# Seven block products in place of eight for half of an output product, in batches 3 to 7

## The chip, the cores and the metric

The kernel runs on one core of a Trainium2 chip. A time is the device time of one execution in microseconds; the time of a kernel is the median over its runs. The profile is of one more execution, taken by the hardware profiler: its span runs from the first to the last instruction. The engines are TensorE (PE, with its weight loads as PEld), VectorE (DVE), ScalarE (ACT), GpSimd (POOL) and SyncE (SP), which issues nearly all transfers.

## What is computed

Random-feature attention for 8 batches of 8 heads (576 tokens, 64 wide), and after it a dense two-layer network over the 4608 tokens that come out:

```
phi(x) = exp(h - max(h)) / sqrt(128),  h = omega x - |x|^2/2
attention = phi(q) (phi(k)^T v) / (phi(q) sum phi(k) + 1e-6)
h = x @ w_in              # 512 -> 2048 (d_ff)
g = h * erf(softplus(h))
out = g @ w_out           # 2048 -> 512
```

Everything is fp32. TensorE is given each number as a high part (rounded to fp32r) and the rest; a product is three matmuls, high x high, high x rest and rest x high.

## The kernel before

Tokens are worked on by batch (576 tokens, as two halves of T = 288), d_ff by two phases of 1024. A matmul has a 128x128 weight and a moving operand of 128x288. A phase (b, ph) has four steps `f0` to `f3`, each making 256 rows of h (a tile hs of 2 row blocks x 2 token halves), and four steps `e0` to `e3` that make the output product of the *phase before*, 128 output rows each. `BLOCKS` gives their order: f0 f1 e0 f2 e1 f3 e2 e3. From batch 2 on the first product (`gemm1`, with the table `PRODUCTS`) is done by a Strassen-like scheme: seven products of blocks in place of eight, with sums of the inputs (tiles xc, split into xh and xl) and of the weights (`make_sums`, tiles wS). The names hA.. and hS.. are PSUM tiles of these seven products; DVE and ACT add them into hs. The output product (`gemm2`, PSUM tiles o..) is plain: for each of 4 output blocks, 2 token halves and 8 row blocks of d_ff three matmuls, 192 in a phase.

Between them stands `chain`: after two steps f, ACT makes softplus and erf of two tiles hs (gs, with a table load ahead of each function), then hs is multiplied by gs (the gate, on DVE or POOL), rounded into gh (DVE or ACT), and the rest hs - gh goes into gl (POOL or DVE).

The program is written down by a planner (`Plan.order`). It gives each operation a due time, counts back from the matmuls with costs written into the source, and lets each engine take the most urgent ready operation; what comes out is one fixed list for each engine. On the chip each engine works through its list in order, and waits by semaphores. Tiles lie in pools of slots (`SLOTS`): 8 for weights (512 KB each, fetched again from device memory for every use), 6 each for gh and gl, 4 for hs, 8 PSUM banks. `CAPS` limits how many PSUM banks one kind of product holds: 3 for h, 2 for o, 6 for the attention.

The attention for later batches (names ppk, ppq, kvp, pt, nd on PE; unk, unq, fk, fq, qh, ql, kh, kl, xs elsewhere) is put between these steps. Batch 7 has none left beside it. In the profile nearly all instructions have line 866, that of the helper which records them; one reads it by tile names.

Of the kernel before, what the change touches and what calls it, by code (L numbers as in the profile page):

```python
# [62 lines left out]
LAG = {"T": 0.35, "A": 0.35, "V": 0.33, "G": 0.33, "S": 0.3}  # L63
SLOTS = dict(w=8, u=2, un=2, f=2, mx=2, sq=2, v=2, qh=1, ql=1, kh=2, kl=2, xs=4, xh=2, xl=2, u2=2,
             hs=4, gs=2, gh=6, gl=6, os=4, ps=8)
# [6 lines left out]
SHARED = ("wrest", "wshift", "wwhole", "wsum", "xsum", "xhigh", "xrest", "gate",  # L72
          "high", "rest")

# [247 lines left out]

BLOCKS = (("f", 0), ("f", 1), ("e", 0), ("f", 2), ("e", 1), ("f", 3), ("e", 2), ("e", 3))
WHOLE = 12
PLAIN = 2
# [29 lines left out]
def build(emit):  # L355
# [3 lines left out]
    seq = [(b, ph) for b in range(B) for ph in range(NPH)]  # L359
    starts = [START0]  # L360
    for b, ph in seq:
        starts.append(starts[-1] + FP * (STEP2 + (STEP1 if b >= PLAIN else STEP1 * 8 / 7))
                      + (NP * PAIR / 2 if b + 1 < B else 0.0))
# [21 lines left out]
    def fetch(u, t, src):  # L385
        pl.op("wfetch", [("S", 0.1, AHEAD)], lambda e: E.fetch(t.ap.bitcast(F32), src()),
              reads=[(stored[u], 0)], writes=[(t, (x, k)) for x in "hl" for k in range(t.shape[1])],
              size=P * t.shape[1] * BW * 8)

    def store(u, t):  # L390
        d = stored[u] = pl.tile("wd" + t.name, "wd" + t.name, t.shape)
        pl.op("wstore", [("S", 0.1, 1e9)], lambda e: E.fetch(d.ap, t.ap.bitcast(F32)),
              reads=[(t, (x, k)) for x in "hl" for k in range(2)], writes=[(d, 0)],
              plan=clock[0] + 10.0, size=P * HW * 8)
# [43 lines left out]

    def make_sums(ph, fp, t0, t1):

        r = pl.tile("gh", f"R{ph}_{fp}", [P, 2, 2, BW], F32, "sr", 1)
# [4 lines left out]
        s = pl.tile("gl", f"S{ph}_{fp}", [P, 4, BW], F32, "ss", 1)  # L446

# [282 lines left out]
    def gemm1(b, ph, fp):  # L730
        where = weights1(b, ph, fp)
        hs = pl.tile("hs", f"hs{b}_{ph}_{fp}", [P, 2, 2, T])
        gran[b, ph, fp] = {"hs": hs}
        u2 = pl.tile("u2", f"u2{b}_{ph}_{fp}", [P, T])

        def place(x):
            return (u2, 0) if x == "U2" else (hs, x)

        def view(x):
            return u2.ap if x == "U2" else hs.ap[:, x[0], x[1], :]  # L740
        for wn, xn, outs in PRODUCTS:
            hp = pl.tile("ps", f"h{wn}{b}_{ph}_{fp}", [P, 512], F32, "moe1")
            product(hp, where, wn, b, XB, xn, 0, 1)
            for to, plus in outs:
                if plus is None:
                    pl.op("hout", [("A", 0.34, -1e9), ("V", 0.38, 0.0)],
                          lambda e, hp=hp, to=to: E.h_out(e, view(to), hp), reads=[(hp, 0)],
                          writes=[place(to)])
                else:
                    pl.op("hadd", [("V", 0.375, -1e9)],  # L750
                          lambda e, hp=hp, to=to, plus=plus: E.h_add(view(to), hp, view(plus)),
                          reads=[(hp, 0), place(plus)], writes=[place(to)])

    macros = [0]

    def chain(b, ph, fps):
# [13 lines left out]
        for fp, g in zip(fps, gr):  # L770
            four = [(g["hs"], (i, t)) for i in range(2) for t in range(2)]
            pl.op("gate", [("V", 1.27, -1e9), ("G", 2.78, GATES if (b, ph) >= EARLY else GATES0)], lambda e, g=g: E.gate(e, g["gs"], g["hs"]),
                  reads=four + [(g["gs"], 0)], writes=four)
            g["gh"] = pl.tile("gh", f"gh{b}_{ph}_{fp}", [P, 2, 2, T], F32R, cap=4 if b < PLAIN or (b, ph) == (PLAIN, 0) else None)
            pl.op("high", [("V", 0.68, -1e9), ("A", 1.08, 3.0)], lambda e, g=g: E.high(e, g["gh"], g["hs"]),
# [3 lines left out]
                  lambda e, g=g: E.rest(e, g["gl"], g["hs"], g["gh"]),  # L779
                  reads=four + [(g["gh"], 0)], writes=[(g["gl"], 0)])  # L780

    def gemm2(b, ph, et):
# [4 lines left out]
        for h in range(2):  # L787
            w = weights2(ph, et, h)
            for t in range(2):
                for fi in range(FT // 2):  # L790
                    f = h * (FT // 2) + fi
                    fp, i = divmod(f, 2)
                    g = gran[b, ph, fp]
                    k = [(w, (x, fi // 2)) for x in "hl"]
                    pl.op("g2", [("T", 3 * COST["mm"], -1e9)],
# [28 lines left out]
    for k, (b, ph) in enumerate(seq):  # L824
        length = starts[k + 1] - starts[k]
        clock[0] = starts[k]
        clock[1] = length / (FP * (STEP2 + STEP1 * (1 if b >= PLAIN else 8 / 7)))
        if not ph:
            for c in range(KH):
                split(b, c)  # L830
        for i, (what, x) in enumerate(BLOCKS):
            if what == "f":
                (plain1 if b < PLAIN else gemm1)(b, ph, x)
                if x % 2:
                    chain(b, ph, (x - 1, x))
# [13 lines left out]
def tile_attention_moe(ctx: ExitStack, tc: tile.TileContext, qT, kT, qN, kN, vP, omT, w1, w2, out):  # L849
# [62 lines left out]
    class Emit:  # L912
# [217 lines left out]
        def gemm2(self, op, w, fi, gh, gl, i, t, f):  # L1130
            b, c = divmod(fi, 2)
            wh, wl = (w.ap[:, b, x, c * P:(c + 1) * P] for x in range(2))
            for x, (l, r) in enumerate(((wh, gh.ap), (wh, gl.ap), (wl, gh.ap))):
                pe.matmul(op.ap[:, :T], lhsT=l, rhs=r[:, i, t, :], start=f == 0 and x == 0,
                          stop=f == FT - 1 and x == 2)

        def o_out(self, e, o, op, t):
# [71 lines left out]
```

## Time and profile before

| | |
|---|---|
| time, median of 3 runs | 1026.38 us (1026.01 to 1029.21) |
| the profiled execution | 1024.2 us, span 1022.4 us |
| busy: PE, PEld | 1005.8 us (98%), 977.8 us (96%) |
| busy: DVE, ACT, POOL | 725.5 us (71%), 688.1 us (67%), 552.3 us (54%) |
| transfers | 254.18 MB, 249 GB/s over the span |
| granted TensorE clock | 1.000 |

Batch 2 begins near 299 us, batch 3 near 420 us, and a batch takes 121.5 us from there to batch 6. Matmuls overlap: one lasts about 0.3 us, but they start 0.13 us apart. A view by windows gives, for each stretch, the busy time of each engine with its instructions, the granted clock, the busy share of the 16 DMA engines and GB/s.

### The profile page before, as it was taken

How to read it: one execution, taken by the hardware profiler on the slowest of the kernel's cores; microseconds unless marked ns; L12 is line 12 of the kernel's file. 1: busy time of each engine (PE TensorE's matmuls, PEld its weight loads, DVE VectorE, ACT ScalarE, POOL GpSimd, SP SyncE). 2: the span in 40 equal slices, each digit the busy share in tenths (PEclk: the TensorE clock that was granted, in tenths of full speed). 3: DMA queues.
4: the chain of work that ended last, by engine and by line, in shares of the span. 5: the costliest groups of instructions: out<-in, count | busy, mean ns of one | idle time of the engine just before them, and what ended most of it. 6: DMA issues, size and time to landing. Idle time of an engine off the chain costs nothing.

```text
span 1022.4 us, 23095 instructions
## 1 busy us (share of the span) xinstructions
PE 1005.8 (98%) x8784; PEld 977.8 (96%) x8784; DVE 725.5 (71%) x1430; ACT 688.1 (67%) x1321; POOL 552.3 (54%) x532
## 2 busy tenths in 40 slices
PE   7999999999999999999999999999999999999998
PEld 7788899999999999999999999999999999999998
DVE  4889889978786677876686767875668756765531
ACT  7979979878685865676677666876657676453340
POOL 6959979879884353835356342752439212343310
PEclk9999999999999999999999999999999999999999
DMA  8676888887776877768776776776866656667761
GB/s 247 201 273 237 287 287 299 286 320 301 276 245 220 306 253 259 246 226 283 247 240 246 274 266 205 246 265 256 281 217 233 220 181 236 226 244 259 274 228 48
DMA packets 80285, 254.18 MB, mean 249 GB/s; under 512 B 9008, under 2 KB 9776, under 8 KB 80176
## 3 DMA queue, kind: packets, MB, share of 16 engines
q1 hardware_dynamic: 80016, 252.12, 71.2%
q8 instruction: 70, 1.15, 0.4%
q10 hardware_dynamic: 160, 0.59, 0.2%
q14 instruction: 39, 0.32, 0.1%
HBM read 218.07 MB, written 34.60 MB: 247 GB/s over the span
## 4 chain that ended last, share of the span: by engine, by line
PE 91%; ACT 3%; DVE 2%; POOL 1%; DMA 1%; issue 0%; SPq 0%; DVEq 0%; POOLq 0%
PE o L866 39%; PE hS L866 15%; PE hA L866 11%; PE h L866 8%; PE nd L866 5%; PE ppk L866 3%; PE kvp L866 3%; PE ppq L866 3%; PE pt L866 2%; ACT fk L866 1%; ACT gs L866 1%; ACT xs L866 1%; DMA uq<-qT 1%; DVE xs L866 0%; DVE pw L866 0%
## 5 line engine op out<-in xcount | busy, mean ns | idle before, releaser
L866 PE MATMUL o<-gh,w 128*128 128x288 f32 x2048 | 445.4, 299 | 0.2 <-DMA w<-wdw 0.2
L866 PEld LDWEIGHTS o<-gh,w 128*128 128x128 f32 x2048 | 338.4, 188 | 5.5 <-issue 0.4
L866 PE MATMUL o<-gl,w 128*128 128x288 f32 x1024 | 301.8, 295 | 0.0
L866 POOL TENSOR_TENSOR hs<-gs,hs 128x576 f32<-128x576 f32 x78 | 124.3, 1617 | 181.1 <-ACT gs L866 118.9
L866 PEld LDWEIGHTS o<-gl,w 128*128 128x128 f32 x1024 | 192.8, 188 | 0.5
L866 PE MATMUL hS<-xh,wS 128*128 128x288 f32 x768 | 186.9, 298 | 0.2 <-ACT fq L866 0.2
L866 POOL TENSOR_TENSOR gl<-hs,gh 128x576 fp32r<-128x576 f32 x80 | 136.7, 1732 | 36.4 <-ACT gh L866 26.1
L866 PE MATMUL hA<-xh,w 128*128 128x288 f32 x576 | 148.1, 298 | 0.0
L866 PEld LDWEIGHTS hS<-xh,wS 128*128 128x128 f32 x768 | 134.3, 188 | 1.1 <-ACT fq L866 0.5
L866 POOL TENSOR_TENSOR unq<-unq 128x288 f32<-128x288 f32 (+2 forms) x67 | 54.5, 815 | 121.6 <-ACT unq L866 75.4
L866 PE MATMUL h<-xh,w 128*128 128x288 f32 x512 | 117.8, 307 | 2.1 <-ACT w L866 1.1
L866 ACT ACT_TABLE_LOAD x92 | 118.0, 1283 | 2.3 <-PEq L1200 0.7
L866 PE MATMUL hS<-xl,wS 128*128 128x288 f32 x384 | 113.4, 295 | 0.0
L866 ACT ACTIVATE fk<-ppk,mxk 128x128 f32<-128x128 f32 x288 | 77.4, 417 | 52.4 <-DVE mxk L866 52.3
L866 PEld LDWEIGHTS hA<-xh,w 128*128 128x128 f32 x576 | 103.3, 188 | 0.0
L866 ACT ACTIVATE xs<-nd,eps 64x288 f32<-64x288 f32 x128 | 63.9, 499 | 48.1 <-PE nd L866 45.8
L866 PEld LDWEIGHTS h<-xh,w 128*128 128x128 f32 x512 | 85.4, 188 | 5.4 <-DVE w L866 1.6
L866 ACT ACTIVATE gs<-hs 128x1152 f32<-128x1152 f32 x64 | 72.9, 1165 | 18.6 <-DVE hs L866 18.2
L866 PE MATMUL hA<-xl,w 128*128 128x288 f32 x288 | 85.2, 296 | 0.0
L866 ACT ACTIVATE fq<-ppq,mxq 128x128 f32<-128x128 f32 x288 | 78.5, 413 | 4.0 <-DVE mxq L866 2.2
L866 PE MATMUL h<-xl,w 128*128 128x288 f32 x256 | 75.8, 296 | 2.2 <-POOL xl L866 2.2
L866 PEld LDWEIGHTS hS<-xl,wS 128*128 128x128 f32 x384 | 72.3, 188 | 0.0
(106 smaller groups left out, 2033.5 us busy)
## 6 DMA issues: line engine op xcount, KB each, us to landing
w<-wdw SPq DMA_DIRECT2D x176, 512.0 KB, 4.5
wS<-wdcS SPq DMA_DIRECT2D x96, 512.0 KB, 4.4
st<-w SPq DMA_DIRECT2D x32, 512.0 KB, 5.6
wdw<-w SPq DMA_DIRECT2D x32, 512.0 KB, 4.3
w<-wdw SPq DMA_DIRECT2D x48, 256.0 KB, 3.7
v<-vP SPq DMA_DIRECT2D x32, 325.0 KB, 5.7
out<-os SPq DMA_DIRECT2D x31, 288.0 KB, 4.1
wdcS<-cS SPq DMA_DIRECT2D x16, 512.0 KB, 4.9
```

The source lines that it names most:

```text
L866: return tc.keep_in_program_order(method(*args, **kwargs))
```

## The change

In batches 3 to 7 the output product of the first phase (ph = 0) is done by the same scheme of seven block products. `operands` takes the four gated tiles hs of the phase in place, makes 16 sums of 128x288 from them (`bsum`, with two spare tiles t2), and splits seven operands (B11, T2, T3, B21, T1, T4, B22; 4 pieces each) into high (`bhigh`, tiles bh in the pool gh) and rest (`brest`, tiles bl in the pool gl): 28 + 28 pieces. The four `high` and four `rest` of these phases, which work on 128x1152, are left out. `block_product` does one of the seven products for two pairs of output blocks: 12 matmuls each into one PSUM tile (bA.., bS..), which DVE (sometimes ACT) then adds to one or two places of the output tile os. That is 168 matmuls in a phase in place of 192. `CUT` lays products 0 to 2 into e0, 3 into e1, 4 and 5 into e2, 6 into e3; in batch 7 `LASTCUT` has 0 and 1, 2, 3 to 6, none.

The weights of these products come as 512 KB columns (wcA from w_out, wcS from its sums), 14 fetches a phase in place of 8. The sums of w_out are made once, in batch 2 (`column_sums`, four times; tiles ct, RT, ST, cST), and stored. Two of the four tiles hs live in the pools gh and gl for these phases (`LENT`). From batch 3 on h may hold 4 PSUM banks, and a block product 3. In `PRODUCTS` the spare tile U2 is replaced by a place in hs that is not filled yet, in all batches that use it; the number of operations stays the same there.

Three places show how the lists change, all in phase (3, 1). **POOL**, from the gate of the third tile on, before:

```order
L866 TENSOR_TENSOR hs3_0_2_6210<-gs3_0_2_6581,hs3_0_2_6210 128x576 x2
L866 TENSOR_TENSOR xc4_0_6709<-xs_4_0_6072 128x288
L866 TENSOR_TENSOR gl3_0_2_6741<-hs3_0_2_6210,gh3_0_2_6714 128x576 x2
L866 TENSOR_TENSOR unk_5_2_6753<-unk_5_2_6753 128x9x32
L866 TENSOR_TENSOR unk_5_2_6753<-unk_5_2_6753 128x9x16
```

and now (the gate stands right ahead of these rows):

```order
L984 TENSOR_SCALAR bhB113_0_6312<-hs3_0_3_6519 128x288
L984 TENSOR_SCALAR bhB113_0_6312<-hs3_0_2_6293 128x288
L984 TENSOR_TENSOR hs3_0_2_6293<-hs3_0_2_6293 128x288
L984 TENSOR_SCALAR bhT23_0_6797<-t23_0_0_6388 128x288
L984 TENSOR_SCALAR bhT33_0_6811<-hs3_0_0_5982 128x288
L984 TENSOR_TENSOR blT23_0_6823<-t23_0_0_6388,bhT23_0_6797 128x288
...
L984 TENSOR_TENSOR hs3_0_2_6293<-t23_0_2_6918,hs3_0_2_6293 128x288
L984 TENSOR_TENSOR blT23_0_6823<-t23_0_2_6918,bhT23_0_6797 128x288
L984 TENSOR_TENSOR hs3_0_2_6293<-hs3_0_2_6293,t23_0_2_6918 128x288
L984 TENSOR_TENSOR t23_0_3_6979<-hs3_0_3_6519 128x288
```

Where one rest of two halves followed the gate, 16 instructions of 128x288 now stand up to the sum t2 of the fourth tile (t23_0_3): 4 roundings, 8 rests (6 of them at the dots) and 4 sums. **DVE**, where it empties the PSUM tiles of f1, before:

```order
L866 TENSOR_TENSOR hs3_1_1_6873<-hA123_1_1_6888,hs3_1_1_6873 128x288
L866 TENSOR_TENSOR hs3_1_1_6873<-hS13_1_1_6909,hs3_1_1_6873 128x288
L866 TENSOR_TENSOR hs3_1_1_6873<-hS13_1_1_6909,u23_1_1_6883 128x288
L866 TENSOR_TENSOR xs_4_2_6905<-nd_4_2_0_0_6861,xs_4_2_6905 64x288
L866 TENSOR_TENSOR hs3_1_1_6873<-hA223_1_1_6919,hs3_1_1_6873 128x288
```

and now:

```order
L984 TENSOR_TENSOR hs3_1_1_6960<-hA123_1_1_6984,hs3_1_1_6960 128x288
L984 TENSOR_TENSOR blT23_0_6823<-t23_0_3_6979,bhT23_0_6797 128x288
L984 TENSOR_TENSOR hs3_1_1_6960<-hS13_1_1_7005,hs3_1_1_6960 128x288 x2
L984 TENSOR_TENSOR hs3_1_1_6960<-hA223_1_1_7015,hs3_1_1_6960 128x288
L984 TENSOR_REDUCE sqq_10_7044<-unq_5_0_6481 128x9
```

The rest of T2's fourth piece, which needs that sum from POOL and its rounding from ACT, now stands ahead of the emptying of hS1. **PE**, at the beginning of e0, before:

```order
L866 MATMUL hS43_1_1_6928<-xh3_0_5710,wS_1_1_1_135_6722 128x288
L866 MATMUL o3_0_0_0_6935<-gh3_0_0_6253,w2_0_0_0_137_6804 128x288
L866 MATMUL o3_0_0_0_6935<-gl3_0_0_6277,w2_0_0_0_137_6804 128x288
L866 MATMUL o3_0_0_0_6935<-gh3_0_0_6253,w2_0_0_0_137_6804 128x288
L866 MATMUL hS43_1_1_6928<-xh3_1_5720,wS_1_1_1_135_6722 128x288
```

and now, there and further down:

```order
L984 MATMUL hS43_1_1_7023<-xh3_0_5750,wS_1_1_1_135_6799 128x288
L984 MATMUL bA113_0_0_7031<-bhB113_0_6312,wcA1100_137_6890 128x288
L984 MATMUL bA113_0_0_7031<-blB113_0_6342,wcA1100_137_6890 128x288
...
L984 MATMUL bS23_0_1_7124<-bhT23_0_6797,wcS201_140_6947 128x288
L984 MATMUL bS23_0_0_7099<-bhT23_0_6797,wcS200_139_6935 128x288
L984 MATMUL bS23_0_0_7099<-blT23_0_6823,wcS200_139_6935 128x288
L984 MATMUL bS23_0_0_7099<-bhT23_0_6797,wcS200_139_6935 128x288
```

The product with B11 begins where the plain one did; the last rows are the fourth piece of T2, 48 instructions after that beginning, 258 after the last matmul of f3 of the phase before.

The core of the diff (the placing into the loop, the plan of the PRODUCTS and the copies of the old functions are cut):

```diff
+CUT = (0, 3, 4, 6, 7)
+LASTCUT = (0, 2, 3, 7, 7)
+BLOCKS2 = 3
+LENT = ("hs", "gh", "gl", "hs")
+MOE1 = 4
+MOE2 = 3
+SUMS2 = ((0, 1), (0, 5), (1, 1), (1, 5))
...
+    def operands(b, ph):
+        gr = [gran[b, ph, fp] for fp in range(FP)]
+        spare = [pl.tile("t2", f"t2{b}_{ph}_{fp}", [P, T]) for fp in range(FP)]
...
+        def total(to, a, c):
+            for fp in range(FP):
+                (d, dk), (x, xk), (y, yk) = place(to, fp), place(a, fp), place(c, fp)
+                pl.op("bsum", [("V", 0.4, -1e9), ("G", 0.75, 3.0)],
+                      lambda e, d=d, x=x, y=y: E.combine(e, d(), x(), y(), -1), reads=[xk, yk], writes=[dk])
...
+                pl.op("bhigh", [("A", 0.44, -1e9), ("V", 0.28, -1e9), ("G", 0.45, 3.0)],
+                      lambda e, h=h, src=src, fp=fp: E.b_high(e, h, src, fp), reads=[key], writes=[(h, fp)])
+                pl.op("brest", [("V", 0.46, -1e9), ("G", 0.78, 3.0)],
...
+        split("B11", b11)
+        total(b12, b12, b11)
+        total("T2", b22, b12)
+        split("T2", "T2")
+        total(b11, "T2", b11)
+        split("T3", b11)
+        split("B21", b21)
+        total(b21, b21, "T2")
+        split("T1", b12)
+        split("T4", b21)
+        split("B22", b22)
...
+        for ep in range(KT // 2):
+            w = column(ph, ep, wn)
+            op = pl.tile("ps", f"b{wn}{b}_{ph}_{ep}", [P, 512], F32, "moe2", MOE2)
+            for f in range(FP):
+                pl.op("g2", [("T", 3 * COST["mm"], -1e9)],
...
+            elif last and blocks2(*last):
+                cut = CUT if k + 1 < len(seq) else LASTCUT
+                for n in range(cut[x], cut[x + 1]):
+                    block_product(*last, n)
...
+            if b == BLOCKS2 - 1 and (ph, i) in SUMS2:
+                ep, h = divmod(SUMS2.index((ph, i)), 2)
+                column_sums(0, ep, h)
```

More of the change, by code (lines that the diff above doesn't have):

```diff
@@ L72 @@
 SHARED = ("wrest", "wshift", "wwhole", "wsum", "xsum", "xhigh", "xrest", "gate",
-          "high", "rest")
+          "high", "rest", "bsum", "bhigh", "brest")
 class Tl:
@@ L360, in build, with blocks2, length2 @@
     starts = [START0]
+    def blocks2(b, ph):
+        return b >= BLOCKS2 and ph == 0
+    def length2(b, ph):
+        return STEP2 * (7 / 8 if blocks2(b - 1 + ph, 1 - ph) else 1)
     for b, ph in seq:
-        starts.append(starts[-1] + FP * (STEP2 + (STEP1 if b >= PLAIN else STEP1 * 8 / 7))
+        starts.append(starts[-1] + FP * (length2(b, ph) + (STEP1 if b >= PLAIN else STEP1 * 8 / 7))
                       + (NP * PAIR / 2 if b + 1 < B else 0.0))
@@ L751, in gemm1 @@
                           lambda e, hp=hp, to=to, plus=plus: E.h_add(view(to), hp, view(plus)),
-                          reads=[(hp, 0), place(plus)], writes=[place(to)])
+                          reads=[(hp, 0), (hs, plus)], writes=[(hs, to)])
     macros = [0]
@@ new lines, in block_product @@
+    def block_product(b, ph, n):
+        wn, xn, outs = PRODUCTS[n]
+        if n == 0:
+            for et in range(KT):
+                o_sb[b, et] = pl.tile("os", f"os{b}_{et}", [P, 2, T])
+        h, l = gran[b, ph][xn]
+        for ep in range(KT // 2):
[3 more added lines that the diff above has]
+                pl.op("g2", [("T", 3 * COST["mm"], -1e9)],
+                      lambda e, w=w, op=op, f=f: E.block_product(op, w, f, h, l),
+                      reads=[(w, (x, f // 2)) for x in "hl"] + [(h, f), (l, f)], writes=[(op, 0)], plan=at())
+            for to, plus in outs:
+                d = o_sb[b, 2 * ep + to[0]]
+                if plus is None:
+                    pl.op("oout", [("V", 0.38, -1e9), ("A", 0.34, -1e9)],
+                          lambda e, d=d, op=op, to=to: E.o_out(e, d, op, to[1]),
+                          reads=[(op, 0)], writes=[(d, to[1])])
+                else:
+                    p = o_sb[b, 2 * ep + plus[0]]
+                    pl.op("oadd", [("V", 0.375, -1e9)],
+                          lambda e, d=d, p=p, op=op, to=to, plus=plus:
+                          E.h_add(d.ap[:, to[1], :], op, p.ap[:, plus[1], :]),
+                          reads=[(op, 0), (p, plus[1])], writes=[(d, to[1])])
@@ L826, in build @@
         clock[0] = starts[k]
-        clock[1] = length / (FP * (STEP2 + STEP1 * (1 if b >= PLAIN else 8 / 7)))
+        clock[1] = length / (FP * (length2(b, ph) + STEP1 * (1 if b >= PLAIN else 8 / 7)))
         if not ph:
@@ L830, in build @@
                 split(b, c)
-        for i, (what, x) in enumerate(BLOCKS):
+        for i, (what, x) in enumerate(BLOCKS if k + 1 < len(seq) else LASTBLOCKS):
             if what == "f":
@@ L1131, in gemm2 @@
             b, c = divmod(fi, 2)
-            wh, wl = (w.ap[:, b, x, c * P:(c + 1) * P] for x in range(2))
+            wh, wl = (w.ap[:, c, x, b * P:(b + 1) * P] for x in range(2))
             for x, (l, r) in enumerate(((wh, gh.ap), (wh, gl.ap), (wl, gh.ap))):
@@ L1135, in gemm2, with block_product, b_high, b_rest @@
                           stop=f == FT - 1 and x == 2)
+        def block_product(self, op, w, f, h, l):
+            a, c = divmod(f, 2)
+            wh, wl = (w.ap[:, a, x, c * P:(c + 1) * P] for x in range(2))
+            for x, (p, r) in enumerate(((wh, h.ap), (wh, l.ap), (wl, h.ap))):
+                pe.matmul(op.ap[:, :T], lhsT=p, rhs=r[:, f, :], start=f == 0 and x == 0,
+                          stop=f == FP - 1 and x == 2)
+        def b_high(self, e, h, src, f):
+            copy(e, h.ap[:, f, :], src())
+        def b_rest(self, e, l, src, h, f):
+            difference(e, l.ap[:, f, :], src(), h.ap[:, f, :].bitcast(F32))
         def o_out(self, e, o, op, t):
```

90 lines of the change are left out of this document (66 added, 24 removed).

## The prediction

> **What bounds the kernel now.** I read the page first, then the windows batch by batch, then the chain that ended last, then the timeline of one hand-off.
>
> ```profile
> PE 1005.8 (98%) x8784; PEld 977.8 (96%) x8784; DVE 725.5 (71%) x1430; ACT 688.1 (67%) x1321; POOL 552.3 (54%) x532
> PE 91%; ACT 3%; DVE 2%; POOL 1%; DMA 1%; issue 0%; SPq 0%; DVEq 0%; POOLq 0%
> 419.80:480.60 60.80, 60.80 (x551) 59.99 (x550) 43.01 (x97) 41.56 (x82) 29.25 (x28) 1.00 0.75 258
> 480.60:541.40 60.80, 60.80 (x548) 59.71 (x547) 43.20 (x91) 41.45 (x77) 30.68 (x30) 1.00 0.70 245
> 940.00:986.00 46.00, 46.00 (x349) 46.00 (x348) 21.82 (x40) 14.84 (x16) 13.48 (x8) 1.00 0.73 246
> 985.78 33.40 PE o L866 x252
> ```
>
> The first row is the page's busy times, the second the chain by engine. The three windows (span, then PE, PEld, DVE, ACT and POOL busy with their counts, the granted clock, the DMA share, GB/s) are the two phases of batch 3 and most of the last phase of batch 7: PE is busy for all of each, at full clock. The last row is a piece of the chain, the end of the program: 252 matmuls one behind the other. So in the stretch that is changed only the number of matmuls counts, as long as nothing else becomes late.
>
> **What is taken away.** The last row prices a matmul: 33.40 / 252 = 0.1325 us. Five phases have 168 in place of 192, 120 matmuls fewer, and 120 x 0.1325 = 15.9 us. The kinds of matmul are the same (128x128 against 128x288), and PE has nothing else taken or added. This is the whole gain; everything below takes from it.
>
> **What is added beside PE, and where it can come to light.** (1) *The hand-off in batches 3 to 6.* In the trace of before it is phase (3, 1):
>
> ```profile
> 464.50 0.29 PE L866 MATMUL hS<-xh,wS 128*128 128x288 f32 x1
> 468.92 2.22 ACT L866 ACTIVATE gs<-gs 128x1152 f32<-128x1152 f32 x2
> 470.17 2.79 POOL L866 TENSOR_TENSOR hs<-gs,hs 128x576 f32<-128x576 f32 x2 [4.16 <-ACT gs L866]
> 493.11 0.30 PE L866 MATMUL o<-gh,w 128*128 128x288 f32 x1
> ```
>
> These are the last matmul of f3, erf, the gate of the third tile and the first matmul of e0. The new POOL list has 16 instructions of 128x288 between that gate, which ends at 472.96, and the sum that T2's fourth piece needs. Their nearest rows, as minimum/median/maximum in ns, and two with a mean:
>
> ```profile
> L866 POOL TENSOR_TENSOR xl<-xs,xh x17: 791/1250/1933, 25.7 to 887.3; 128x288 fp32r<-128x288 f32 x17
> L866 POOL TENSOR_TENSOR xc<-xs,xc x8: 802/861/1327, 261.8 to 891.5; 128x288 f32<-128x288 f32 x8
> L866 POOL TENSOR_SCALAR xh<-xs x8: 431/552/1004, 25.0 to 884.8; 128x288 fp32r<-128x288 f32 x5, 128x576 fp32r<-128x576 f32 x3
> L866 POOL TENSOR_TENSOR xl<-xs,xh 128x288 fp32r<-128x288 f32 x17 | 19.9, 1189 | 0.4 <-ACT xh L866 0.3
> L866 POOL TENSOR_TENSOR xc<-xs,xc 128x288 f32<-128x288 f32 x8 | 7.7, 963 | 1.7 <-DVE xc L866 1.6
> ```
>
> Eight rests, four sums, four roundings: at the minima 8 x 0.79 + 4 x 0.80 + 4 x 0.43 = 11.2 us, at the means (0.55, the median, for a rounding) 9.5 + 3.9 + 2.2 = 15.6 us, at the maxima 15.5 + 5.3 + 4.0 = 24.8 us. The sum is there at 484.2, 488.6 or 497.8; rounding on ACT and rest on DVE take about 1.6 us more (an estimate: 0.43 for the rows of ACT like hs<-hA, 0.72 as the mean of DVE's xc<-xs,xc, and the semaphores between):
>
> ```profile
> L866 ACT ACTIVATE hs<-hA 128x288 f32<-128x288 f32 x23 | 9.6, 417 | 34.8 <-PE hA L866 34.7
> L866 DVE TENSOR_TENSOR xc<-xs,xc 128x288 f32<-128x288 f32 x16 | 11.6, 722 | 0.2 <-POOL xc L866 0.2
> ```
>
> PE wants the piece 48 instructions behind the beginning of e0, of which 6 are transposes; e0 itself begins three matmuls later in the new list, at 493.5, so that is about 493.5 + 6.4 = 499.9. But DVE is first to feel it, since the rest stands ahead of the emptying of hS1 in its list: hS1 is done 9 matmuls ahead of e0, at 492.3, and behind it stand some 12 instructions of about 0.45 us up to the first emptying of a block product. That one frees the bank that PE's fourth block tile takes, near 499.5. So the piece must be through by about 494.5, the sum from POOL by 492.9. At the means there are 4.3 us to spare; at the maxima it is 4.9 us late, 24.5 us over five batches. I take 0.3 us a batch, 1.5 in all, since the sums lie nearer the means; a gain has no way in.
>
> Here the two SBUF engines hinder each other: the same DVE subtraction reads quite differently from PSUM and from SBUF.
>
> ```profile
> L866 DVE TENSOR_TENSOR hs<-hS,hs x96: 441/457/460, 302.4 to 985.8; 128x288 f32<-128x288 f32 x96
> L866 DVE TENSOR_TENSOR xc<-xs,xc x16: 447/518/1555, 287.6 to 873.1; 128x288 f32<-128x288 f32 x16
> ```
>
> The Trainium skill (SBUF — State Buffer, "Who interferes with whom") says that DVE and GpSimd share one pair of ports as an exclusive lock, which a DVE instruction with two SBUF inputs takes against a GpSimd one that reads SBUF; the spread of the second row, and none in the first, agree. By that rule the 24.8 us of the maxima cannot come together: POOL's 11.2 us and DVE's own gate and ten small ones of that stretch, some 6 us, one after the other give 17 us, the sum from POOL is there at 490, and the loss is 0.
>
> (2) *Batch 7* has the same hand-off without attention. From f3's end PE reaches T2's fourth piece after 213 matmuls, 28.2 us. DVE forms that piece's sum only behind the emptying of f1's last tile, 174 matmuls or 23.1 us in; then come POOL's rounding and four DVE instructions, about 4 us. A microsecond is left; it is within the 0.3 above, and its bound within the 4.9.
>
> (3) *DVE's load.* Per batch it gets about 9 more emptyings, 12 rests, 6 sums and 3 roundings, and loses 2 of `high` and 1 of `rest`:
>
> ```profile
> L866 DVE TENSOR_TENSOR os<-o,os 128x288 f32<-128x288 f32 x64 | 28.9, 454 | 60.5 <-PE o L866 59.9
> L866 DVE TENSOR_TENSOR xl<-xs,xh 128x288 fp32r<-128x288 f32 x5 | 6.3, 1257 | 1.4 <-POOL xh L866 1.4
> L866 DVE CAST gh<-hs 128x1152 fp32r<-128x1152 f32 x19 | 19.5, 1043 | 0.0
> L866 DVE TENSOR_TENSOR gl<-hs,gh 128x1152 fp32r<-128x1152 f32 x24 | 42.0, 1754 | 7.2 <-ACT gh L866 7.2
> ```
>
> 9 x 0.45 + 18 x 0.45 to 1.26 + 3 x 0.5 - 3.8 is 10 to 24 us on top of 86.2 (the two windows of batch 3), of 118: 81 to 94%. It still fits, as ACT's 20 more roundings of 0.42 us do, so no term of its own; what crowding costs is in the bounds of (1).
>
> (4) *Transfers.* A column of 512 KB now feeds 12 matmuls, 1.6 us; before, 512 KB fed 24. Phase (b, 1) carries 245 GB/s x 60.8 us = 14.9 MB, plus six columns, 3.1 MB: 18.0 MB in 57.6 us, 313 GB/s. Batch 2 gets 8 fetches and 8 stores, 8.4 MB, on 258 x 121 = 31.2 MB: 327 GB/s. What has been reached:
>
> ```profile
> 290.00:350.00 60.00, 59.77 (x533) 58.56 (x534) 40.03 (x89) 43.59 (x82) 29.93 (x28) 1.00 0.74 262
> 350.00:411.00 61.00, 61.00 (x554) 59.91 (x552) 46.43 (x98) 40.26 (x81) 28.73 (x28) 1.00 0.76 254
> 100.00:160.00 60.00, 59.19 (x584) 55.70 (x583) 52.23 (x101) 52.93 (x110) 50.71 (x56) 1.00 0.86 303
> 340.00:350.00 10.00, 10.00 (x101) 9.76 (x99) 3.44 (x11) 9.44 (x10) 4.55 (x7) 1.00 0.99 375
> w<-wdw SPq DMA_DIRECT2D x176, 512.0 KB, 4.5
> w<-wdw SPq DMA_DIRECT2D x48, 256.0 KB, 3.7
> ```
>
> 303 GB/s was carried for 60 us with PE nearly full, at a share of 0.86, and 375 for 10 us with PE full. If nothing above 303 lasts, a phase (b, 1) takes 59.4 us, 1.8 more than planned, 9 in five, and batch 2 takes 130.7, 9.7 more: 19 us. If it lasts as the short stretch does, nothing. The eight slots hold some 12 us of supply against a landing of 4.5 us (the columns' rows are 2 KB, like those of the 256 KB fetches, which land no later), so I take 1 us for the phases and 1.5 for batch 2.
>
> (5) *The sums of batch 2* are 16 instructions on DVE and 19 on POOL, like those for w_in, of which these rows are the longest:
>
> ```profile
> L866 DVE TENSOR_TENSOR cS<-S,cS 128x512 fp32r<-128x512 f32 x11 | 14.0, 1285 | 0.6 <-POOL cS L866 0.5
> L866 POOL TENSOR_TENSOR R<-w 128x512 f32<-128x512 f32 x8 | 13.2, 1659 | 0.0
> ```
>
> So under 21 and 32 us go into 121 us in which the two windows of batch 2 show 86 and 59 busy: hidden. The two tiles in other pools, the bank limits and U2's new place cost no instruction.
>
> **Sum.** 15.9 - 1.5 - 1 - 1.5 = 11.9 us off the profiled execution's own 1024.2 (span 1022.4): 1012.3. The median of the runs shown is 2.2 us above that execution; against it the forecast is 1026.4 - 11.9 = 1014.5 us.
>
> **Rivals.** *A, nothing comes to light:* all of 15.9 us, 1010.5; the even PE windows and the spare 4.3 us speak for it, the spread of the POOL rows against. *B, the hand-off takes PE's place as bound:* POOL's sixteen are late in every batch and DVE's emptyings stand behind them. It eats the gain when a batch loses 3.2 us, that is when the sum comes at 496.1, 23.1 us after the gate, 1.45 us an instruction; up to the maxima it costs 24.5 us, and the middle of that stretch, with the 2.5 of transfers, is 1026.4 - 15.9 + 20.2 + 2.5 = 1033, slower. For it speaks that the median rest on POOL is 1.25 already, against it the low sums and roundings. *C, transfers:* a sustained limit of 303 GB/s gives 1026.4 - 15.9 + 19 + 1.5 = 1031; halfway, 1022. For it: more per microsecond than any 60 us show; against it, the 375. *D, the change isn't what it says:* the PE list has just 120 matmuls fewer; no chance given.
>
> **Chances.** Forecast with A 0.77 (forecast 0.57, A 0.20), B 0.12, C 0.11. No change is within 0.3%, 3 us. Forecast and A are faster but for 0.03, the forecast's far end, that is no change; C is split in three; B is slower but for 0.02: faster 0.74 + 0.04 = 0.78, same 0.03 + 0.04 + 0.02 = 0.09, slower 0.10 + 0.03 = 0.13. The range runs from 1009, A with 1.5 us of scatter, to 1026, the near part of B and C; the forecast's own is 1011 to 1018.
>
> **What would show it.** Right: PE full in batches 3 to 7, phases (b, 1) near 57.6 us, DVE over 80% there. B right: PE idle at e0, with hS, bA or bS released by DVE or POOL, or DVE's bl rows waiting for ACT bh. C right: PE idle released by DMA w, ct or wc, share near 1 in phases (b, 1). The forecast is wrong if PE idles over 3 us in a batch from 3 on, or if batch 2 grows by more than 3 us.

## The result

The change takes 1017.93 us (median of 4 runs, 1016.57 to 1018.86), the kernel before 1026.20 (4 runs, 1025.52 to 1029.21): the ratio is 0.9913, 95% interval 0.9889 to 0.9937. That is 8.3 us less, where 11.9 had been forecast and 15.9 are the bare matmuls. The time lies in the forecast's own range, at its upper end.

Page of the changed kernel, busy times and the chain by engine:

```profile
PE 996.0 (98%) x8664; PEld 965.5 (95%) x8664; DVE 793.4 (78%) x1591; ACT 703.7 (69%) x1388; POOL 667.6 (66%) x691
PE 85%; ACT 4%; POOL 4%; DMA 3%; DVE 3%; issue 1%; SPq 0%; POOLq 0%; ACTq 0%; DVEq 0%
```

PE has its 120 matmuls fewer, and is still the bound: 98% busy. But its share of the chain fell from 91 to 85%, and DVE has 68 us more of work, POOL 115. The windows of (3, 0), (3, 1) and (4, 1) now (span, then PE, PEld, DVE, ACT and POOL, the granted clock, the DMA share, GB/s):

```profile
421.60:485.30 63.70, 61.91 (x549) 59.88 (x547) 49.72 (x108) 43.34 (x91) 39.81 (x45) 1.00 0.82 278
485.30:543.40 58.10, 58.10 (x523) 56.67 (x522) 50.50 (x113) 36.66 (x81) 41.12 (x47) 1.00 0.88 294
604.50:665.90 61.40, 58.62 (x524) 56.72 (x523) 55.17 (x120) 39.76 (x86) 44.52 (x49) 1.00 0.83 287
```

Phase (3, 1) is what was promised: PE busy for all of it, 58.1 us. In (3, 0), where no block product runs, PE is 1.8 us short of the span; in (4, 1) it is 2.8 us short, so that this phase is no shorter than it was. What PE waited for from batch 2 on (us in all, times, longest), now and then before:

```profile
PE bA L984 <- DVE os L984: 2.0, 2, 1.1
PE nd L984 <- DVE ql L984: 1.2, 2, 0.8
PE ppk L984 <- ACT fk L984: 0.7, 1, 0.7
PE nd L984 <- DVE hs L984: 0.5, 1, 0.5
PE hS L984 <- ACT fq L984: 0.5, 1, 0.5
```

```profile
PE hS L866 <- ACT fq L866: 0.2, 1, 0.2
PE o L866 <- DMA w<-wdw: 0.2, 1, 0.2
```

No wait in the first list is for an operand bh or bl, and none is for a transfer. Most are for DVE, for rows that empty PSUM or make an operand of the attention (ql). The idle time of PE understates a stop: matmuls overlap, so from the start of one to the start of the next a stop costs some 0.15 us more (an estimate: they last 0.30 us and start 0.13 apart). The table shows where. It gives the length of each phase, from its first matmul hA to that of the next, read from PE's timeline; the columns at the right are four of the experiments below.

| phase | before | change | no sums | sums early | four banks | more traffic |
|---|---|---|---|---|---|---|
| start of (2, 0) | 296.72 | 299.44 | 300.11 | 298.36 | 299.65 | 298.65 |
| (2, 0) | 61.34 | 61.52 | 61.59 | 61.44 | 61.53 | 61.50 |
| (2, 1) | 60.87 | 60.62 | 61.00 | 63.35 | 60.62 | 60.62 |
| (3, 0) | 60.45 | 63.72 | 61.00 | 63.41 | 63.34 | 63.44 |
| (3, 1) | 60.79 | 58.13 | 58.17 | 58.18 | 57.09 | 58.10 |
| (4, 0) | 60.66 | 61.03 | 61.01 | 61.10 | 62.62 | 61.07 |
| (4, 1) | 60.74 | 61.39 | 61.46 | 60.55 | 57.06 | 65.11 |
| (5, 0) | 60.39 | 60.94 | 60.89 | 60.95 | 62.63 | 60.94 |
| (5, 1) | 61.60 | 58.16 | 58.16 | 58.09 | 57.11 | 58.64 |
| (6, 0) | 61.12 | 61.13 | 61.09 | 61.02 | 62.66 | 61.14 |
| (6, 1) to the end | 174.50 | 167.35 | 167.40 | 168.05 | 167.47 | 169.67 |

A phase (b, 1) should lose 24 x 0.1325 = 3.2 us. (3, 1) and (5, 1) do, within 0.6 us, and the last two together, within 0.8. Against that stand 2.7 us ahead of batch 2, 3.3 in (3, 0), 3.8 in (4, 1) (3.2 of gain not seen, and 0.65 of loss), and 0.9 in (4, 0) and (5, 0) together. The other phases are within 0.3 us of what was planned, and the two profiled executions end 5.7 us apart.

**Phase (3, 0)** carries the end of the column sums. DVE's timeline there (start, us, operation), and the two matmuls of the attention that wait:

```profile
418.74 1.90 DVE L984 TENSOR_TENSOR RT<-ct 128x512 f32<-128x512 f32 x1
...
422.83 2.20 DVE L984 TENSOR_TENSOR ST<-RT 128x256 f32<-128x256 f32 x2
424.96 1.64 DVE L984 TENSOR_TENSOR ST<-ST,RT 128x256 f32<-128x256 f32 x1
...
426.89 1.28 DVE L984 TENSOR_TENSOR ST<-RT,ST 128x256 f32<-128x256 f32 x1
428.10 0.44 DVE L984 TENSOR_TENSOR hs<-hS,hs 128x288 f32<-128x288 f32 x1
...
430.85 1.95 DVE L984 TENSOR_TENSOR cST<-ST,cST 128x512 fp32r<-128x512 f32 x1
432.73 0.55 DVE L984 TENSOR_TENSOR ql<-pt,qh 128x384 fp32r<-128x384 f32 x1
```

```profile
428.60 0.40 PE L984 MATMUL nd<-qh,kh 128*128 128x288 f32 x1 [0.51 <-DVE hs L984]
...
433.33 0.40 PE L984 MATMUL nd<-ql,kh 128*128 128x288 f32 x1 [0.81 <-DVE ql L984]
```

Six passes of 0.6 to 1.95 us (the row of 2.20 is two) stand in DVE's list between emptyings of 0.45, a seventh of 0.93 follows at 434.48, in a crowded place, where the next batches' attention and the new batch's first product meet. A third matmul nd waits 0.41 us for ql at 448.39, after the sums.

**Phase (4, 1)** has three stops. One is for the attention's exponentials (fk), two are of block products that wait for a PSUM bank:

```profile
640.30 0.37 PE L984 MATMUL ppk<-wq,uk 64*128 64x128 f32 x1 [0.74 <-ACT fk L984]
...
657.77 0.40 PE L984 MATMUL bA<-bhT,wcA 128*128 128x288 f32 x1 [0.92 <-DVE os L984]
...
660.75 0.40 PE L984 MATMUL bA<-bhT,wcA 128*128 128x288 f32 x1 [1.12 <-DVE os L984]
```

```profile
656.90 0.82 DVE L984 TENSOR_TENSOR os<-bS,os 128x288 f32<-128x288 f32 x2 [0.28 <-PE bS L984]
...
659.33 1.01 DVE L984 TENSOR_REDUCE sqq<-ppq 128x3 f32<-128x384 f32 x2
660.25 0.44 DVE L984 TENSOR_TENSOR os<-bA,os 128x288 f32<-128x288 f32 x1
```

Each block product waits for the emptying of the one just ahead of it, as if there were one bank. DVE is not late with the first emptying: it stood idle for 0.28 us until PE had finished bS. With the second it is late by some 0.6 us: the bA ahead is done near 659.6, and two maxima (sqq, 1.01 us) still stand ahead of the emptying. A product with a bank of its own has no such wait: in (3, 1) none stops. In the program's list the banks are these: tiles have fixed banks, and the last bS of product 4 and both bA of product 5 have the same one. One other bank holds an hS whose matmuls are half done, and six hold tiles ppq of the attention, until their maxima (sqq) and exponentials (fq) are made. The group of PE's matmuls into ppq, with first and last start at its end, in (4, 1) and then in (3, 1), where nothing waits:

```profile
L984 PE MATMUL ppq<-wq,uq x18: 272/272/373, 653.6 to 655.6; 64*128 64x128 f32 x18
...
L984 PE MATMUL ppq<-wq,uq x18: 272/272/373, 533.3 to 538.9; 64*128 64x128 f32 x18
```

In (3, 1) the list puts four tiles first and two 5 us later, and block products between them; in (4, 1) all six come at one go. From start to start the three stops cost some 3.3 us of the phase's 3.8, the two for a bank 2.4 of them.

**The start.** Of the 2.7 us ahead of batch 2, most come about at one place where both kernels still have the same list (the first 250 instructions of DVE are the same in both): the 30th matmul of the first product starts 0.7 us later than before, the 60th 2.8 us. The windows there, changed kernel first:

```profile
50.00:55.00 5.00, 3.15 (x29) 2.46 (x28) 4.51 (x10) 3.03 (x8) 4.59 (x9) 0.89 0.68 229
55.00:60.00 5.00, 4.88 (x25) 4.03 (x25) 3.64 (x9) 2.34 (x10) 4.20 (x6) 0.50 0.30 92
```

```profile
50.00:55.00 5.00, 2.92 (x29) 2.32 (x28) 4.90 (x11) 3.03 (x9) 4.75 (x7) 1.00 0.82 266
55.00:60.00 5.00, 4.87 (x40) 4.58 (x41) 4.78 (x13) 3.46 (x15) 3.60 (x6) 1.00 0.50 114
```

The granted clock is halved from 53.9 us on, for 6.8 us, and PE gets 25 instructions done in the second window where it got 40. Of 42 timed runs of the kernel before on three chips, 41 have a mean clock of 0.994 to 0.998; the one with 1.000 is the fastest of all, 1024.23 us, and the profiled execution has 1.000 too. So that trace is better than the kernel's usual run by about the 2.2 us that lie between it and the median, and medians are what is compared from here on.

### The profile page after: what moved, and what is told of

It reads as the page before. It is cut to its first block, busy times and chain, and to the rows that moved or that the text cites. A ratio compares the mean times of both kernels' runs of the same rounds, so it can differ in the third digit from the quotient of the medians.

```text
span 1016.6 us, 23361 instructions
## 1 busy us (share of the span) xinstructions
PE 996.0 (98%) x8664; PEld 965.5 (95%) x8664; DVE 793.4 (78%) x1591; ACT 703.7 (69%) x1388; POOL 667.6 (66%) x691
## 4 chain that ended last, share of the span: by engine, by line
PE 85%; ACT 4%; POOL 4%; DMA 3%; DVE 3%; issue 1%; SPq 0%; POOLq 0%; ACTq 0%; DVEq 0%
PE o L984 26%; PE hS L984 14%; PE hA L984 11%; PE h L984 8%; PE bS L984 6%; PE nd L984 5%; PE bA L984 5%; PE ppk L984 3%; PE kvp L984 3%; PE ppq L984 3%; PE pt L984 2%; POOL unq L984 1%; DMA unk<-kN 1%; ACT fq L984 1%; DMA st<-w 1%
## 5 line engine op out<-in xcount | busy, mean ns | idle before, releaser
L984 PE MATMUL o<-gh,w 128*128 128x288 f32 x1408 | 306.4, 300 | 0.2
L984 PEld LDWEIGHTS o<-gh,w 128*128 128x128 f32 x1408 | 232.4, 188 | 4.5 <-DVE os L984 0.4
L984 PE MATMUL o<-gl,w 128*128 128x288 f32 x704 | 207.2, 294 | 0.0
L984 PEld LDWEIGHTS o<-gl,w 128*128 128x128 f32 x704 | 132.6, 188 | 0.5
L984 DVE TENSOR_TENSOR hs<-hS,hs 128x288 f32<-128x288 f32 x240 | 104.6, 451 | 33.1 <-PE hS L984 29.0
L984 POOL TENSOR_TENSOR gl<-hs,gh 128x576 fp32r<-128x576 f32 x52 | 85.7, 1673 | 15.5 <-ACT gh L984 9.4
L984 POOL TENSOR_TENSOR unq<-unq 128x144 f32<-128x144 f32 (+2 forms) x67 | 55.2, 825 | 38.6 <-ACT unq L984 30.6
```

What stands on the lines that cost most here:

```text
L984: return tc.keep_in_program_order(method(*args, **kwargs))
```

## The experiments

The program's order comes from the planner, which knows banks, slots and costs. Each edit below makes it write new lists for all engines, so a time holds the edit and the lists that follow from it; placement alone can move a time by some 2 us, as the third one shows.

**1. The sums of columns without their use.** The sums are made and stored in batch 2; all output products are plain.

```
-BLOCKS2 = 3
+BLOCKS2 = 8
...
-            if b == BLOCKS2 - 1 and (ph, i) in SUMS2:
+            if b == 2 and (ph, i) in SUMS2:
```

> The kernel before, with only the second part of the change: the four sums of w_out in batch 2 are made and stored, but no phase uses them, every output product stays plain. Theory: the sums are not hidden, as the prediction had it; the last of them runs on DVE and POOL into the first step of batch 3, and the emptying of PSUM behind it on DVE comes late. Then this is 2 to 3 us slower than the kernel before (1028.5 to 1029.5), with PE waiting for DVE near 430 us. If the transfers of batch 2 are the cost (8.4 MB more), PE waits for DMA w in batch 2 and the loss is about the same. If the sums are hidden, as predicted, it is 1026.2.

Measured: 1028.91 us against 1026.53 before, ratio 1.0023 (1.0013 to 1.0032). The sums cost 2.4 us by themselves. In the trace phase (3, 0) takes 63.98 us, batch 2 is no longer than before, and from the start of batch 2 to the end of (3, 0) PE waits for no weight; in (3, 0) it waits for DVE, 1.9 us for ql and 0.5 for hs, all between 427 and 435 us. So nothing there points to the 8.4 MB of transfers.

**2. The change without the sums.** The blocks fetch plain columns of w_out where they should have sums, so the output is not the product; all matmuls, transfers to PE and operands are as in the change.

```
-  "S2": (("T", ph, ep, 0), 0), "S3": (("T", ph, ep, 0), 1),
-  "S1": (("T", ph, ep, 1), 0), "S4": (("T", ph, ep, 1), 1)}[wn]
+  "S2": (("2", ph, 2 * ep), 0), "S3": (("2", ph, 2 * ep), 1),
+  "S1": (("2", ph, 2 * ep + 1), 0), "S4": (("2", ph, 2 * ep + 1), 1)}[wn]
...
-            if b == BLOCKS2 - 1 and (ph, i) in SUMS2:
+            if False:
```

> The changed kernel without the sums of w_out: the block products fetch columns of w_out itself in place of the sums (so the output is another one); number and size of the fetches from batch 3 on stay the same. Theory (the sums cost 2.5 us): 1015.4 us, PE without waits near 430 us. If the sums were hidden: 1017.9.

Measured: 1015.76 us (1014.67 to 1016.87), ratio 0.9893 (0.9871 to 0.9914), 2.2 us under the change. Two experiments from opposite sides agree, and the table puts the gain in (3, 0): 61.00 in place of 63.72, while batch 2 itself is no shorter. The waits of bA for DVE's os stay, so they have another cause.

**3. The sums at other places.**

```
-SUMS2 = ((0, 1), (0, 5), (1, 1), (1, 5))
+SUMS2 = ((0, 1), (0, 4), (0, 7), (1, 3))
```

> The change with the four sums of columns at other places of batch 2: behind the second, fifth and eighth block of its first phase and the fourth of its second, so that none runs into batch 3. In the trace of the change only the last sum, whose instructions run from 418 to 435 us beside the first blocks of batch 3, stands where time is lost (3.1 us in that phase, none in batch 2). Theory (the place of the last sum costs, not the sums as such): 2 to 3 us less than the change, 1015 to 1016, as without any sums. Rival (32 more instructions on two loaded engines cost the same wherever they stand): 1017.5 to 1018.5.

Measured: 1020.29 us (1019.30 to 1022.24), ratio 0.9947 (0.9930 to 0.9964): 2.4 us *more* than the change. The edit did not move what it was meant to move. Neither theory gave that. The view of the tile RT, the first step of a sum, at the border to batch 3, and the waits of PE in (2, 1):

```profile
L984 DVE TENSOR_TENSOR RT<-ct x2: 779/1350/1922, 419.5 to 420.2; 128x512 f32<-128x512 f32 x2
```

```profile
PE hS L984 <- DVE hs L984: 1.9, 1, 1.9
```

The last sum still starts at 419.5; only the third went forward, from 377.6 to 365.8, and PE waited there (63.35 in that phase). The place in the program text is not the place in time: a sum begins when its tiles R and S find slots in the pools gh and gl, which the gated tiles fill most of the time. That this is the reason is read from the source and not shown by a run. So this run says nothing for or against "the place costs"; that it cost 2.4 us more for another sum at another busy place speaks for it.

**4. All four tiles hs in their own pool.**

```
-LENT = ("hs", "gh", "gl", "hs")
+LENT = ("hs", "hs", "hs", "hs")
```

> The changed kernel with all four gated tiles of a phase in the pool of hs, none in the pools of gh and gl. Theory: the four slots are held until the last operand is split, so f0 and f1 of the next phase have no slot and cannot cover the making of the operands; each of the five hand-offs then loses about 10 us (the operands need some 20 us after the gate, two steps e give 12.7): 1060 to 1080 us. If the hand-off has slack enough anyway, 1018 to 1022.

Measured: 1062.68 us (1061.23 to 1064.85), ratio 1.0355 (1.0334 to 1.0377), 45 us over the change. PE's first waits:

```profile
PE bS L984 <- DMA wcS<-wdcST: 9.3, 8, 1.9
PE bA L984 <- DVE xs L984: 7.3, 4, 2.1
```

As expected in size. That the four slots of hs stay taken until the operands are made, so that the next h begins late, is how the source reads; the trace shows the stops that came of it.

**5 to 7. The limits of banks.** Both old limits, then each alone.

```
-MOE1 = 4
-MOE2 = 3
+MOE1 = 3
+MOE2 = 2
```

Run 6 has only the second of these edits, run 7 only the first.

> The changed kernel with the bank limits of before: 3 PSUM banks for h and 2 for a block product, in place of 4 and 3. Theory: what is left of the loss in batches 3 to 7 are late emptyings on DVE (PE waits for os at 656 to 661 us), and one bank less makes each of them dearer: 3 to 8 us slower than the change, 1021 to 1026. If banks are no part of it: 1018.

> The change with the old limit of two banks for the block products (the four banks for products of the first GEMM stay). Both old limits together gave 1034.4, 16.5 us over the change. Theory: a block product lasts 1.6 us of PE and its bank is free only after one or two emptyings by DVE, so two banks leave no room for a late emptying, and this limit carries most of the 16.5: 1028 to 1033. Rival: the limit of the first GEMM carries it: 1018 to 1022 here.

> The change with the old limit of three banks for the products of the first GEMM (three banks for the block products stay). Theory (the block products' limit carries the 16.5 us): 1019 to 1023 here. Rival (the first GEMM's limit carries it): 1028 to 1033.

| banks for h, for block products | time | ratio to before |
|---|---|---|
| 4, 3 (the change) | 1017.93 | 0.9913 (0.9889 to 0.9937) |
| 4, 2 | 1028.93 | 1.0029 (1.0019 to 1.0039) |
| 3, 3 | 1033.21 | 1.0078 (1.0057 to 1.0099) |
| 3, 2 | 1034.44 | 1.0082 (1.0063 to 1.0101) |

With the old limits the change would be slower than the kernel before. I had expected 3 to 8 us, and then that the block products' limit carries most. Both miss: each limit alone takes back the whole gain (11 and 15 us), and together they cost hardly more than the worse one. PE's longest lists of waits from batch 3 on, with two banks for blocks, then with three for h:

```profile
PE bS L984 <- DVE os L984: 2.8, 2, 1.4
PE o L984 <- DVE gl L984: 2.6, 3, 1.2
```

```profile
PE bA L984 <- DVE os L984: 6.3, 6, 1.3
PE bA L984 <- DMA wcA<-wdw: 4.1, 2, 2.3
```

With three banks for h, the stops of (4, 1) come in three batches, six in all, though the block products have their three banks. Its PE also waits 7.1 us for weights, 4.1 for wcA and 3.0 for w, where the change waits for none. The list has changed: in (3, 1) too, all tiles ppq now come ahead of the two bA.

```profile
L984 PE MATMUL ppq<-wq,uq x18: 271/272/373, 531.4 to 533.4; 64*128 64x128 f32 x18
```

So a limit acts through the order of the whole list. How much of the 15 us is banks on the chip and how much the order that the planner then writes stays open.

**8. The limits of banks without the change.**

```
-CAPS = dict(st=2, wt=2, cv=2, att=6, moe1=3, moe2=2)
+CAPS = dict(st=2, wt=2, cv=2, att=6, moe1=4, moe2=3)
...
-BLOCKS2 = 3
+BLOCKS2 = 8
...
-SUMS2 = ((0, 1), (0, 5), (1, 1), (1, 5))
+SUMS2 = ()
```

> The kernel before (no block products, no sums of columns) with the new limits of banks alone: four for the first GEMM, three for the second. Theory (the limits give room for the emptyings of the block products; the old list has PE waiting 0.4 us in all of batches 2 to 7): 1024.5 to 1026.5, no gain that can be told. Rival (the banks are worth something by themselves and the change's 8.5 us are partly theirs): 1021 to 1023.

Measured: 1035.76 us (1034.07 to 1038.05), ratio 1.0088 (1.0070 to 1.0106), slower by 9 us. Neither theory gave that. The trace shows where the loss is: the first hA of batch 2 is at 310.83, 14.1 us later than before, and from there to the end it takes 722.1 us, before 722.4. My edit puts the limits on batches 0 and 1 too, where the weights are still made in PSUM tiles (pw); the change does not. That this is what delays them is read from the source. Some of the 14.1 us will be the clock: 20.5 us ahead of batch 2 run at half the granted clock, none in the trace of before. For batches 2 to 7 the theory holds: the plain list gains nothing from more banks. In these runs they are worth something only to the block products.

**9. Another bank for the block products.**

```
-MOE2 = 3
+MOE2 = 4
```

> The change with four banks in place of three for the block products. With two it is 11 us slower. Theory (what is left of PE's waits in the last three batches of hand-offs is bA waiting for DVE's emptying os, 2.0 us in the trace, and it goes with another bank): 1015 to 1016.5. Rival (three are enough, the fourth is taken from attention, whose nd already waits 1.7 us for its emptyings): 1018 to 1021.

Measured: 1017.24 us (1016.70 to 1018.47), ratio 0.9909 (0.9894 to 0.9925). PE's waits from batch 2 on, all of them:

```profile
PE nd L984 <- DVE ql L984: 0.8, 1, 0.8
PE nd L984 <- DVE hs L984: 0.5, 1, 0.5
PE hS L984 <- ACT fq L984: 0.5, 1, 0.5
```

and the group ppq in (4, 1):

```profile
L984 PE MATMUL ppq<-wq,uq x18: 272/272/373, 653.1 to 665.5; 64*128 64x128 f32 x18
```

The waits of bA are gone, and two of the six ppq come 10 us later, behind the block products. The stop for fk is gone with them. (4, 1) with (5, 0) takes 119.7 us in place of 122.3: so the three stops were worth these 2.6 us; this run does not part them. But the other pairs of phases are 0.5 us longer each, and the median is just 0.7 us under the change's, which the scatter of the two does not tell from nothing. It lies between what theory and rival gave.

**10. All rests of the operands on POOL, and 11. both.**

```
-                pl.op("brest", [("V", 0.46, -1e9), ("G", 0.78, 3.0)],
+                pl.op("brest", [("G", 0.78, -1e9)],
```

> The change with all rests of the operands (28 pieces of 128x288 a batch) on POOL, where 16 of them were before and DVE had 12. Theory (DVE's load is what delays its emptyings, and POOL's hand-off has room): DVE loses 12 x 0.7 = 8 us a batch, POOL gets 12 x 0.88 = 11 us, the time falls by 1 to 3 us, to 1015 to 1017. Rival B of the prediction (POOL's list between the last gate and T2's fourth piece has 4.3 us of reserve at most): with up to 5 more rests ahead of the last sum it is 0 to 3 us late in each of five batches, 1020 to 1030, with PE waiting for DVE or POOL at bS or bA.

> The change with both, four banks for the block products and all rests on POOL. If both theories hold (emptyings that come late for lack of a bank and for DVE's load), 1012 to 1014.5, ahead of the change by 3 to 6 us. If one alone is worth something, its own figure; if neither, 1018 or more.

Measured: 1019.55 us (1018.74 to 1021.69), ratio 0.9932 (0.9916 to 0.9947), and with four banks as well 1018.92 (1017.13 to 1022.95), ratio 0.9929 (0.9911 to 0.9947). The first is 1.6 us over the change, so my theory of DVE's load fails. The time comes near the rival's 1020, but not for its reason: no stop of bS or bA is for DVE or POOL. The run does not press POOL where the rival says it must: up to the last sum of (3, 1) its list has 12 rests in place of 8, but fewer roundings and sums, and 12.4 us of work where the change has 12.0. PE's longest waits, and the group ppq in (4, 1), are

```profile
PE hA L984 <- ACT fk L984: 2.1, 2, 1.4
```

```profile
L984 PE MATMUL ppq<-wq,uq x18: 272/272/373, 654.4 to 663.2; 64*128 64x128 f32 x18
```

No wait there is for an operand. The stops of bA for os are gone here too, but not because DVE has less to do: in this list too the last ppq come behind the block products. The traces of the changed kernel, of three banks for h, of four for blocks and of this one agree, and so do those without sums, with the sums early and with more traffic: in (3, 1), (4, 1) and (5, 1) bA stops where six ppq stand ahead of it, and not where four do. A wait for the attention's exponentials (fk) took the place of the stops. Two edits that each remove the visible wait leave the time where it was.

**12. More traffic.** Every second fetch of a column comes with a copy of 512 KB inside device memory, for which nobody waits: 18 MB more.

```
+        if not ep:
+            c = pl.tile(f"wdx{count[0]}", f"wdx{count[0]}", [P, 2, 2, BW])
+            pl.op("wextra", [("S", 0.1, AHEAD)], lambda e: E.fetch(c.ap, d.ap[:, :, k]),
+                  reads=[(d, 0), (d, 1)], writes=[(c, 0)], plan=clock[0])
```

> The change with every second column fetch of w_out accompanied by a copy of the same 512 KB inside DRAM that nobody waits for: 35 copies, about 18 MB more read and as much written, most of it in the phases (b, 1) and batch 3 to 7. Theory (DVE's crowding and the sums of batch 2 hold back what is missing; transfers have room): the same time, 1018, at most 1020. Rival C of the prediction (a sustained limit just above what the change carries): each copy pushes the columns behind it back by about 1.7 us at the 303 GB/s of the long stretch, 35 x 1.7 = 59 us of queue, of which a fifth to all comes to light: 1030 or more, with PE waiting for wc by DMA.

Measured: 1026.54 us (1022.03 to 1030.36, 10 runs), ratio 1.0000 (0.9982 to 1.0017), 8.6 us over the change. Phase (3, 1) of this run, and PE's waits from batch 3 on:

```profile
483.50:541.80 58.30, 58.30 (x524) 56.88 (x523) 50.21 (x114) 37.07 (x83) 41.30 (x47) 1.00 0.96 337
```

```profile
PE ppk L988 <- ACT fk L988: 2.9, 1, 2.9
...
PE bS L988 <- DMA wcS<-wdcST: 1.4, 1, 1.4
```

Two things follow. The bound of rival C does not exist: 337 GB/s, copies included, lasted for 58 us with PE busy in all of it, 34 above the 303 that the prediction took for the largest stretch, and 43 above what the change carries there (294). But transfers are not free room either. ACT's timeline in (4, 1) says what the 2.9 us are:

```profile
639.86 0.68 ACT L988 ACTIVATE unk<-unk 128x576 f32<-128x576 f32 x1 [2.88 <-DMA unk<-kN]
```

A load of the attention's input landed 7.9 us after its issue, in the change 5.8; a copy had been issued 3.3 us ahead of it, and PE stood at the end of the chain; behind that stop the granted clock is 0.50 for 3.4 us. That phase takes 65.11 us, and in batch 7 PE waits 1.8 us for weights (wcS, wS). This execution is 2 us faster than the median, so a part of the 8.6 us is not in the trace. My theory said 1020 at most, so it was wrong on the size of the reserve; rival C's 1030 was not reached either.

## Why the prediction was right or wrong

*What bounds the kernel, and the gain.* Right. 120 matmuls fewer, PE still at 98%, and of five phases four show their 3.2 us, two within 0.6 and the last two within 0.8 together.

*(1) The hand-off.* It was safe, as the middle of its bounds had it, and its price was not needed; that the time came out close was luck. From the timelines of (3, 1), the gate of the third tile, POOL's next rows, the last sum of T2, its rest and the first matmul that takes T2:

```profile
474.64 2.79 POOL L984 TENSOR_TENSOR hs<-gs,hs 128x576 f32<-128x576 f32 x2 [4.37 <-ACT gs L984]
479.91 1.03 POOL L984 TENSOR_SCALAR bhB<-hs 128x288 fp32r<-128x288 f32 x2 [2.48 <-DVE hs L984]
...
493.24 0.96 POOL L984 TENSOR_TENSOR t<-hs 128x288 f32<-128x288 f32 x1 [0.39 <-DVE hs L984]
...
496.64 0.45 DVE L984 TENSOR_TENSOR blT<-t,bhT 128x288 fp32r<-128x288 f32 x1
...
502.06 0.38 PE L984 MATMUL bS<-bhT,wcS 128*128 128x288 f32 x1
```

From the gate's end at 477.43 to the end of the sum at 494.20 are 16.8 us; 15.6 had been worked out from means of other rows. But POOL works in only 12.0 of them, little more than the 11.2 of the minima, and stands idle in the other 4.7, most of it until DVE has made a tile (2.5 us ahead of the first rounding, 1.1 and 0.4 ahead of two sums). So the prediction took the sixteen instructions 3.6 us too dear and had no term for POOL's own waits, and the two errors nearly cancel; (5, 1) shows the same, 12.0 us of work in 16.8. DVE takes the rest at 496.64 with no idle time ahead of it, the piece is through at 497.1, and PE takes T2's first piece at 502.1. The 4.3 us to spare of the prediction end at another point, where POOL's sum is needed, and were not measured. PE stops for no operand in any of the five batches, and the 1.5 us set aside did not fall due. The rule cited for it (the Trainium skill, SBUF — State Buffer, "Who interferes with whom") gave a sum at 490 and a loss of 0; taking off the gate's own shift of 4.5 us, the sum is there at 489.7. The trace agrees with that outcome, but it does not show POOL held up by the lock: the 490 had 6 us of DVE's instructions standing in POOL's way, and the trace has POOL 0.8 us over its minima and waiting for tiles. Rival B is refuted by the trace of the change; the run with 28 rests on POOL adds little, since it loads that stretch hardly more.

*(3) DVE's load.* The figure was right (49.72 + 50.50 of the 121.8 us of batch 3's two windows, 82%, where 81 to 94 were predicted), and it fits, as predicted. But what crowding costs had been put into the bounds of the hand-off, and it showed elsewhere: in (3, 0), with the sums (below). The two stops of bA in (4, 1) look like DVE's in the list of waits, and were taken for its load at first; the rows of ppq, over all these lists, show that it is the banks, though a busy DVE makes the second of them longer.

*(5) The sums.* This is the step that failed: "hidden" was wrong by 2.2 to 2.4 us, measured twice. The instructions are as small as predicted, 20.9 us for DVE's 16 in all, against batch 2, which kept its length; but they do not spread over it. Seven of the 16 are the last sum, 10 us of DVE between 418.7 and 435.4, on the border to batch 3, where they take up to 1.95 us each, and emptyings stand behind them.

*(4) Transfers.* The sum was right that 303 GB/s is no limit. Of the 2.5 us set aside, PE's waits show nothing. Rival C is refuted as a limit; as a reserve, 18 MB more were too much.

*The bank limits and the lent tiles.* "Cost no instruction", in the same step, was true and the wrong question, and here the prediction has its largest gap: PSUM was not asked about. Two of the three stops of (4, 1) are for banks. And without the limits or the lent tiles the change is 16.5 or 45 us slower: they are what lets the gain come to light at all. The Trainium skill (Perfetto Trace Analysis, "Optimizing Tensor Performance") says that independent groups of matmuls should go round through different PSUM banks, so that emptying one overlaps the next. The table of limits agrees, as far as times can that hold the new lists too: fewer banks for as many emptyings cost 11 to 16.5 us.

*Sum.* From the gain of 15.9 us the median keeps 8.3. Of the 7.6 lost, 2.2 are the sums and 3.8 stand in (4, 1) of the trace, of which 2.6 go with a fourth bank and the list that follows from it; 0.9 in (4, 0) and (5, 0) show no wait that I can name, and some 0.7 stay open. The forecast had set 4.0 aside, for the hand-off and for transfers, where nothing was lost. That the time still lies in its own range is in part luck: the losses are others and nearly twice as large. It had also said that PE idle over 3 us in a batch from 3 on would make it wrong. Batch 4 comes to 2.8 us, and lost 3.8.

No version here beats the change by more than the scatter. Four banks for the block products is the best that computes the product, 1017.24.

## What to carry to other kernels

When a product is cut into more and smaller ones, count the PSUM banks at the worst place and not only the work: who else holds banks there, and how many are left to go round. A wait for an emptying is not yet a sign that the emptying engine is late; look whether it stood idle ahead of it. What seems to be bookkeeping in a change (bank limits, tiles in another pool) is worth an experiment before it is costed at nothing; here it was larger than the whole gain. And removing the visible wait is no gain when the new list has another stop elsewhere: two runs did so, and the time did not move.

## What the runs showed of the hardware

The granted clock halves after a short stop of PE, in some executions of the same piece and not in others. In the changed kernel a stop of 1.75 us is followed by a window at 0.50; before, stops of 1.68 and 0.54 us at the same place by one at 1.00:

```profile
54.51 0.61 PE L984 MATMUL h<-xl,w 128*128 128x288 f32 x1 [1.75 <-POOL xl L984]
```

```profile
53.93 0.40 PE L866 MATMUL h<-xl,w 128*128 128x288 f32 x1 [1.68 <-POOL xl L866]
55.13 0.40 PE L866 MATMUL h<-xl,w 128*128 128x288 f32 x1 [0.54 <-POOL xl L866]
```

It costs about 2.1 us here (from 0.7 us late at the 30th matmul of the first product to 2.8 at the 60th). In the traces of the experiments each such stretch within the program lasts 3.4 or 6.8 us. From batch 2 on each begins in a stop of PE or at most 1.5 us behind its end, and these stops lasted 1.7 to 4.9 us (2.9 with more traffic, 2.0 in experiment 11); a stop of 1.9 us with the sums early is followed by none. The Trainium skill (TensorE: Matmul & The Clock Gate, "HAM oscillation — how this bites in real kernels") warns of idle gaps over about 3.4 us; this trace has the halved clock behind a shorter one. For a kernel at 98% PE this means that one profiled execution can lie 2 us beside the median for no reason in the program.
